# Pointwise weights loaded as 256 + 128 rows around the first input block, and one weight piece evicted by two engines

## The chip, the cores and the metric

The kernel runs on one core of one Trainium2 chip. The metric is the device time of one execution in microseconds (us); the median of several runs is compared.

## What is computed

A depthwise separable convolution with a 1x1 depthwise kernel, in bf16. `x` is (1, 384, 384, 384), that is 147,456 pixels of 384 channels; `dw` is (1, 1, 384) and `pw` is (384, 384):

```python
out = x * dw[0, 0][None, None, None, :]      # k = 1: no neighbours, no padding
return jnp.einsum('bhwc,cd->bhwd', out, pw)
```

So it is one matrix product of 147,456 x 384 by 384 x 384, whose weights are `pw` with row c scaled by `dw[c]`.

## The kernel before

**Tiling.** The pixels are cut into 288 supertiles of 512. Chunks of 1 to 10 supertiles are loaded by one DMA each into three rotating buffers X; the first two chunks, x0 and x1, are one supertile each, the next two have two, then one has four, and from there on most have ten. For each supertile VectorE (DVE in the profile) transposes 32x32 blocks of 32-bit words from X to T (L369; for the very first supertile block by block, L367), the tensor engine (PE) multiplies, and ScalarE (ACT) evicts the result from PSUM to O (L429), from where SyncE's queue (SP) stores it.

**The main stream.** `supertile(s, rv)` issues 12 steps `(b, par)` of four matmuls each, one for each quarter q of the partitions, all at L225. The weights are the moving operand `w_r[:, b, par, :]`, T the stationary one. Results go to the PSUM buffer PS[0] for even supertiles and PS[1] for odd ones, one bank per q. `w_first` lists which weight evictions a step of an even supertile waits for: those of pieces 0 to 3 before step (0,0), piece 4 before (4,0), piece 5 before (4,1), which are the ninth and eleventh steps. `s_tb` makes steps (1,0) and (2,0) wait for blocks 1 and 2 of the first transpose.

**The weights.** Because the transpose works on pairs of channels, the rows of `pw` are spread to another order and scaled by `dw` on PE. `pw` lies in `raw` as three parts k of 128 rows. For each k and r in 0, 1, a pair of matmuls (L275, v = 0 and 1, each on 64 rows of the array and each into a bank of its own) makes weight *piece* i = 2k + r in two PSUM banks: pieces 2 and 3 in PS[0], the others in PS[1]. The left operand `sel_w` is a 0/1 selection times `dw`, made by DVE (L400) from a transposed `dw` row (L255). `times` repeats a pair: the same matmuls again into the same banks, with the piece's mark `s_w` after the last. `w_out(i)` evicts piece i from PSUM into `w_r` (L385); the engine is `w_eng[i]`, 0 for DVE and 1 for ACT, and `s_wr[e]` counts what each engine has evicted. Pieces 4 and 5 use the banks of pieces 0 and 1 and wait for their eviction (L272).

**Order at the start.** Each engine works through its instructions in the order written.
- SP's queue: `pw` part 0 (L179), `pw` parts 1 and 2 (L180), x0, x1 and the following chunks (L133). The first stores are held by 28 waits on `s_pw` (L195).
- PE: `idle_work(4)`, the `dw` row, `idle_work(2)`, the six pieces, then the main stream. `idle_work(n)` issues n sets of four matmuls on constants (L242); nothing reads what they write.
- DVE: the selection, `sel_w`, its piece, then the transposes of supertiles 0 and 1.
- ACT: its pieces in order, then the output evictions.
- GpSimd (POOL) copies some weights for the last supertile once all pieces are out (`w_all`, L329 to L333).

## Time and profile before

| | |
|---|---|
| median of 5 runs | 573.95 us (573.62 to 574.03) |
| profiled execution, its own time | 574.21 us |
| its span (first to last profiled instruction) | 572.2 us |
| granted clock in the page | 9 in all 40 slices (90% of full speed or more) |
| PE / PEld (weight loads) | 566.8 us (99%) / 417.0 us (73%) |
| DVE / ACT / POOL | 507.3 us (89%) / 418.7 us (73%) / 13.9 us (2%) |
| DMA | 226.88 MB, mean 397 GB/s |
| first matmul of the main stream | 6.39 us |

PE is the matmul row and PEld its weight loads, which overlap it; matmul ends are modelled. L12 is line 12 of the kernel. An entry such as "0.3 <-ACT w_r L385" says that the engine stood for 0.3 us until the instruction named released it. The chain of waits follows the work that ended last back to its start. The timeline merges equal instructions that follow one another. SPq and ACTq are the DMA issues of those engines.

### The profile page before, as it was taken

How to read it: one execution, taken by the hardware profiler on the slowest of the kernel's cores; microseconds unless marked ns; L12 is line 12 of the kernel's file. 1: busy time of each engine (PE TensorE's matmuls, PEld its weight loads, DVE VectorE, ACT ScalarE, POOL GpSimd, SP SyncE). 2: the span in 40 equal slices, each digit the busy share in tenths (PEclk: the TensorE clock that was granted, in tenths of full speed). 3: DMA queues.
4: the chain of work that ended last, by engine and by line, in shares of the span. 5: the costliest groups of instructions: out<-in, count | busy, mean ns of one | idle time of the engine just before them, and what ended most of it. 6: DMA issues, size and time to landing. Idle time of an engine off the chain costs nothing.

```text
span 572.2 us, 29707 instructions
## 1 busy us (share of the span) xinstructions
PE 566.8 (99%) x13843; PEld 417.0 (73%) x13843; DVE 507.3 (89%) x588; ACT 418.7 (73%) x298; POOL 13.9 (2%) x41
## 2 busy tenths in 40 slices
PE   8999999999999999999999999999999999999997
PEld 5777777777777777777777777777777777777774
DVE  6899899899999999999999999999999999999995
ACT  6777777777777777777777777777777777777775
POOL 2042000000000000000000000000000000000000
PEclk9999999999999999999999999999999999999999
DMA  8999999999999999999999999999999999997877
GB/s 343 428 389 422 424 417 425 434 425 416 431 420 424 380 399 430 399 381 396 427 394 383 419 422 414 395 412 428 388 390 423 410 380 395 425 396 301 341 286 255
DMA packets 26740, 226.88 MB, mean 397 GB/s; under 512 B 1385, under 2 KB 7274, under 8 KB 22890
## 3 DMA queue, kind: packets, MB, share of 16 engines
q1 hardware_dynamic: 25796, 225.91, 97.5%
q10 hardware_dynamic: 934, 0.89, 0.4%
q14 instruction: 9, 0.07, 0.0%
q8 instruction: 1, 0.02, 0.0%
HBM read 113.54 MB, written 113.25 MB: 396 GB/s over the span
## 4 chain that ended last, share of the span: by engine, by line
PE 99%; ACT 0%; issue 0%
PE ps L225 98%; ACT w_r L385 0%; PE ps L242 0%; PE ps L310 0%; PE ps L298 0%; PE ps L275 0%; ACT O L424 0%; PE ps L255 0%
## 5 line engine op out<-in xcount | busy, mean ns | idle before, releaser
L225 PE MATMUL ps<-w_r,T 32*128 32x384 bf16 x13776 | 559.8, 321 | 0.3 <-ACT w_r L385 0.3
L369 DVE STREAM_TRANSPOSE T<-X 128x384 uint32<-128x384 uint32 x571 | 499.4, 878 | 55.8 <-DMA X<-in_x_dram 2.9
L225 PEld LDWEIGHTS ps<-w_r,T 32*128 32x128 bf16 x13776 | 414.4, 93 | 145.7 <-issue 0.6
L429 ACT CAST O<-ps 128x1536 bf16<-128x1536 f32 x286 | 411.7, 1440 | 146.4 <-PE ps L225 146.4
L339 POOL COPY Xk<-Xl 32x256 bf16<-32x256 bf16 x16 | 6.3, 394 | 0.0
L338 POOL COPY Xk<-Xl 32x128 bf16<-32x128 bf16 x16 | 4.6, 288 | 25.2 <-DMA Xl<-in_x_dram 24.4
L385 ACT CAST w_r<-ps 128x768 bf16<-128x768 f32 x5 | 3.6, 818 | 0.9 <-PE ps L275 0.9
L333 POOL COPY raw<-w_r 32x768 bf16<-32x768 bf16 x4 | 3.3, 820 | 6.5 <-ACT w_r L385 6.4
L242 PE MATMUL ps<-const-bfloat16-1.0 32*128 32x384 bf16 x24 | 2.3, 512 | 1.1 <-PEq L454 1.1
L275 PE MATMUL ps<-raw 64*128 64x384 bf16 x16 | 2.6, 466 | 0.1
L341 ACT ACT_TABLE_LOAD x1 | 1.3, 1283 | 1.5 <-PEq L454 1.5
L275 PEld LDWEIGHTS ps<-raw 64*128 64x128 bf16 x16 | 0.8, 111 | 2.2 <-DMA raw<-in_pw_dram 1.2
L420 DVE CAST O<-ps 128x384 bf16<-128x384 f32 x2 | 1.0, 552 | 1.4 <-PE ps L225 1.4
L369 DVE STREAM_TRANSPOSE T<-Xl 128x384 uint32<-128x384 uint32 x2 | 1.8, 882 | 0.2
L242 PEld LDWEIGHTS ps<-const-bfloat16-1.0 32*128 32x128 bf16 x24 | 0.6, 117 | 1.4 <-issue 1.4
L390 DVE TENSOR_REDUCE sel<-eye 128x64 f32<-128x128 bf16 x1 | 0.3, 290 | 1.5 <-POOL eye L320 1.5
L352 DVE STREAM_TRANSPOSE T<-Xk 128x384 uint32<-128x384 uint32 x2 | 1.2, 578 | 0.5 <-PE ps L225 0.4
L424 ACT CAST O<-ps 128x384 bf16<-128x384 f32 x2 | 1.0, 480 | 0.7 <-PE ps L310 0.7
L310 PE MATMUL ps<-raw,T 128*128 128x384 bf16 x8 | 1.5, 327 | 0.0
L385 DVE CAST w_r<-ps 128x768 bf16<-128x768 f32 x1 | 1.0, 958 | 0.5 <-PE ps L275 0.5
L424 DVE CAST O<-ps 128x384 bf16<-128x384 f32 x2 | 1.1, 558 | 0.1
L419 ACT CAST O<-ps 128x384 bf16<-128x384 f32 x2 | 0.9, 482 | 0.5 <-PE ps L225 0.5
(14 smaller groups left out, 5.1 us busy)
## 6 DMA issues: line engine op xcount, KB each, us to landing
X<-in_x_dram SPq DMA_DIRECT2D x26, 3840.0 KB, 22.2
out_dram<-O SPq DMA_DIRECT2D x26, 3840.0 KB, 28.2
X<-in_x_dram SPq DMA_DIRECT2D x3, 1536.0 KB, 19.5
out_dram<-O SPq DMA_DIRECT2D x4, 768.0 KB, 8.3
out_dram<-O SPq DMA_DIRECT2D x2, 1536.0 KB, 14.0
X<-in_x_dram SPq DMA_DIRECT2D x1, 2304.0 KB, 21.2
out_dram<-O SPq DMA_DIRECT2D x1, 2304.0 KB, 12.1
X<-in_x_dram SPq DMA_DIRECT2D x4, 384.0 KB, 4.9
```

What stands on the lines that cost most here:

```text
L225: mm = nc.tensor.matmul(PS[s][:, q, :D], lhsT=Ts[s][32 * q : 32 * q + 32, b, par::2], rhs=w_r[32 * q : 32 * q + 32, b, par, :], start=(b, ...
L242: nc.tensor.matmul(PS[0][:, 2 * (i % 2) + i // 2, :D], lhsT=ones[32 * i : 32 * i + 32, 0:P], rhs=ones[32 * i : 32 * i + 32, :], start=True ...
L275: mm = nc.tensor.matmul(PS[(k + 1) % 2][:, 2 * r + v, :D], lhsT=sel_w[64 * v : 64 * v + 64, k, r, :, :].rearrange("p q w -> p (q w)"), rhs ...
L310: mm = nc.tensor.matmul(PS[1][:, m, :D], lhsT=Tk[:, P * (m + 2) : P * (m + 3), par], rhs=w_k[:, par, :], start=False, stop=par == 1,)
L333: nc.gpsimd.tensor_copy(w_k[quads[n]], w_r[quads[n], n]).then_inc(s_wk)
L338: nc.gpsimd.tensor_copy(Xk[quads[n], g:8:4, :], x_b).then_inc(s_xk)
L339: nc.gpsimd.tensor_copy(Xk[quads[n], 8 + g : 24 : 4, :], Xl[quads[g], :, 64 * n : 64 * n + 64]).then_inc(s_xk)
L341: nc.scalar.copy(warm[:, s : s + 1], nc.const_aps.tensor(0.0, [P, 1], F32)).then_inc(s_a[s])
L369: ins = nc.vector.transpose(out=Tw[:, 3 * h : 3 * h + 3], in_=Xw[:, :, j, 96 * h : 96 * h + 96].rearrange("p k (b w) -> p b k w", w=32),)
L385: o = nc.vector.tensor_copy(out, in_) if e == 0 else nc.scalar.copy(out, in_)
L424: o = (nc.scalar.copy if n % 2 else nc.vector.tensor_copy)(Ov[:, n, j, :], PS[s][:, n, :D])
L429: a = nc.scalar.copy(Ov[:, :, j, :], PS[s][:, :, :D])
```

## The change

`pw`'s parts 0 and 1 come in one first DMA, counted by `s_pw`; then x0; then part 2, counted by `s_pw2`, for which PE now waits before k = 2 and not before k = 1. One more set of idle matmuls is issued, piece 3's pair is issued twice, and those of pieces 4 and 5 are issued once. Piece 3 is evicted by two engines: bank 0 by ACT in its old place, bank 1 by DVE between blocks 0 and 1 of the first transpose. The counts that others wait for follow. In total the same bytes are loaded by as many DMAs.

```diff
         w_eng = [1, 0, 1, 1, 1, 1]
-        w_all = [(s_wr[e], w_eng.count(e)) for e in range(2)]
+        w_all = [(s_wr[0], 2), (s_wr[1], 5)]

         nc.scalar.dma_start(dw_row[:], dw.rearrange("a e c -> a (e c)")).then_inc(s_dw, 16)
-        nc.sync.dma_start(pw_n[:, 0], pw[0:P, :]).then_inc(s_pw, 16)
-        nc.sync.dma_start(pw_n[:, 1:3], pw[P:C, :].rearrange("(k p) d -> p k d", p=P)).then_inc(s_pw2, 16)
+        nc.sync.dma_start(pw_n[:, 0:2], pw[0 : 2 * P, :].rearrange("(k p) d -> p k d", p=P)).then_inc(s_pw, 16)
         load_x(0)
+        nc.sync.dma_start(pw_n[:, 2], pw[2 * P : C, :]).then_inc(s_pw2, 16)
...
-        w_first = {(0, 0): [(0, 1), (1, 3)], (4, 0): [(1, 4)], (4, 1): [(1, 5)]}
+        w_first = {(0, 0): [(0, 2), (1, 3)], (4, 0): [(1, 4)], (4, 1): [(1, 5)]}
...
-        idle_work(2)
+        idle_work(3)
         nc.tensor.wait_ge(s_pw, 16)
-        times = {(2, 0): 2, (2, 1): 2}
+        times = {(1, 1): 2}
         for k in range(3):
-            if k == 1:
+            if k == 2:
                 nc.tensor.wait_ge(s_pw2, 16)
             nc.tensor.wait_ge(s_sw, k + 1)
...
                         nc.vector.transpose(out=Tw[:, b], in_=x_b).then_inc(s_tb if b else s_t[0][0])
+                        if b == 0:
+                            w_out(3, 1)
                     continue
...
-        def w_out(i):
+        def w_out(i, bank=0):
             e, k, r = w_eng[i], i // 2, i % 2
             out, in_ = w_r[:, 2 * k : 2 * k + 2, r, :], w_ps(i)
+            if i == 3:
+                out, in_ = out[:, bank], in_[:, bank]
+                e = 1 - bank
             o = nc.vector.tensor_copy(out, in_) if e == 0 else nc.scalar.copy(out, in_)
```

## The prediction

> **What bounds the kernel now.** I read the page first: its chain of waits and its groups of instructions.

> ```profile
> PE 99%; ACT 0%; issue 0%
> PE ps L225 98%; ACT w_r L385 0%; PE ps L242 0%; PE ps L310 0%; PE ps L298 0%; PE ps L275 0%; ACT O L424 0%; PE ps L255 0%
> ...
> L225 PE MATMUL ps<-w_r,T 32*128 32x384 bf16 x13776 | 559.8, 321 | 0.3 <-ACT w_r L385 0.3
> ```

> The main stream of matmuls (L225) is 559.8 us of a span of 572.2, and once it runs it never waits: its whole idle time is the 0.3 us before its first matmul, ended by a weight eviction on ACT. So the change can move the end in three ways only: the stream starts earlier or later, it stalls, or its matmuls run slower.

> Next, the chain in order of time, asked for the first 12 us (start, duration, what):

> ```profile
> 3.51 0.52 PE ps L275 x2
> 4.03 0.02 issue
> 4.05 2.21 ACT w_r L385 x3
> 6.26 0.14 issue
> 6.39 5.68 PE ps L225 x133
> ```

> The stream starts at 6.39, 0.14 after ACT's third eviction (pieces 0, 2 and 3, chained from 4.05). All four pieces must be out before it: supertile 0 writes the PSUM buffer that holds pieces 2 and 3.

> Last, the timeline of the start-up (start, duration, engine, work, idle before it and its releaser), and of DVE at 9 to 10.3 us:

> ```profile
> 3.48 0.16 PEld L275 LDWEIGHTS ps<-raw 64*128 64x128 bf16 x4 [0.74 <-DMA raw<-in_pw_dram]
> 4.05 3.61 ACT L385 CAST w_r<-ps 128x768 bf16<-128x768 f32 x5 [0.93 <-PE ps L275]
> 4.07 0.20 PEld L275 LDWEIGHTS ps<-raw 64*128 64x128 bf16 x4 [0.44 <-DMA raw<-in_pw_dram]
> 4.37 0.96 DVE L385 CAST w_r<-ps 128x768 bf16<-128x768 f32 x1 [0.48 <-PE ps L275]
> 5.53 0.70 DVE L367 STREAM_TRANSPOSE T<-X 128x128 uint32<-128x128 uint32 x3 [0.20 <-DMA X<-in_x_dram]
> ...
> 9.22 1.58 DVE L369 STREAM_TRANSPOSE T<-X 128x384 uint32<-128x384 uint32 x2 [0.89 <-DMA X<-in_x_dram]
> ```

> DVE is done with piece 1 at 5.33 and stands 0.20 until x0 lands at 5.50, while ACT still has piece 3 to do. At 9.22 DVE again has only just got its input: the third supertile's X.

> **The change, part by part.** The sum is made on the profiled run: 574.21 us, its span of 572.20 and 2.01 around it. That is 0.26 above the median of 573.95, so a shift found here is taken off the median.

> *First load, 192 KB for 96.* Before, 96 KB issued at 0.95 landed 2.0 later (2.95), and the 192 KB issued at 1.41 landed 2.6 later (4.03). Bounds for 192 KB issued first: 2.95 and 0.95+2.6=3.58. By packets: the DMA view counts 139 up to 2.50 us, 14 of them under 512 B, about the 128 of the first load, which landed 0.45 later; up to 2.98 it counts 273, 17 of them small, the 256 that the new load has. 2.98+0.45=3.43, or a little under: I take 3.4. The row from landing to matmul is 4.03 to 4.10, so the pieces could start at 3.47; before they started at 3.51, held by sel_w (DVE L400, the first ending at 3.36). The load costs nothing; at its upper bound, 0.14.

> *A third idle_work set.* Each set takes about 0.3 (2.55, then 2.85), so it is issued at about 3.17 and its streaming ends at 3.49 to 3.55 (the last quadrant started late, at 2.91). Beside the wait for the load it costs 0 to 0.04; I charge 0.02.

> *The wait before k=1 taken away.* It ended at 4.03 and the matmuls ran at 4.10. But a pair of L275 takes 0.32 at that clock and the pair before started at 3.78, so 4.10 is when PE was free anyway. The gap of 0.44 on PEld is a hidden one. Gain: nothing.

> *Piece 3 issued twice.* Its pair at 4.42 is repeated at 4.74, so its mark moves from 4.97 to about 5.29. ACT comes to piece 3 at 5.43 and DVE later, so they hide it. Without that cover it would cost up to 0.32.

> *Piece 3 split.* ACT's evictions start 0.69 apart (4.05, 4.74, 5.43). Bank 0 is 128x384; the nearest rows are ACT's output evictions of that shape, 480 and 482 ns: ACT ends at 5.43+0.48+0.02=5.93 for 6.25. Bank 1 goes to DVE behind piece 1 (ends 5.33+0.02) and block 0. DVE's rows for 128x384 out of PSUM are 552 and 558 ns.

> *x0 behind 192 KB for 288.* Issued at 1.41 for 1.87, so up to 0.46 earlier; or by bytes, 98 KB at the 294 GB/s of the stretch from 2.5 to 5.5, 0.33 earlier. That is 5.04 to 5.17 for 5.50; unmoved is the upper bound. Below 5.35 it no longer counts, as DVE isn't free. Block 0 then starts at 5.35, bank 1 0.23 later (blocks started at 5.53 and 5.76) at 5.58, and ends at 6.14; if it overlaps the end of piece 1 by the 0.08 that consecutive DVE rows show, 6.06. I take 6.10. If x0 doesn't move: 5.53+0.23+0.56=6.32.

> *The start.* The last release is DVE's at 6.10 for ACT's at 6.25; 0.14 to the first matmul as before, and 0.03 for the wait on ACT's count that now follows it: 6.27 for 6.39, **0.12 earlier** (0.2 earlier to 0.1 later between the ends).

> *pw's last 96 KB behind x0.* It stands where x0 stood, with the same bytes up to its end: 5.5. Bounds: 96 KB behind x0's earliest 5.04 at 294 GB/s, 5.37; or behind an unmoved x0 at the pace of the old second load (192 KB in 1.08 after the first, so 0.54), 6.04. This wait is new, and in PE's queue all of the main stream stands behind it. 5.55+0.07=5.62, then two pairs (the doubled ones are gone) of 0.32 at the old clock: PE is free at 6.26, just inside 6.27. At the upper bound 6.04+0.07+0.64=6.75, 0.36 later than before.

> *Behind them on ACT:* pieces 4 and 5 at about 6.1 to 6.95 and 6.8 to 7.65; the stream asks for them 8 and 10 steps of 0.163 after its start, 7.57 and 7.90. Hidden with 0.25 to spare.

> *Blocks 1 and 2 and the next transpose on DVE* come about 0.3 later against piece 1's end than they could: 6.05, 6.25 and 6.45, ending by 7.0. The stream asks 0.33, 0.65 and 0.98 after 6.27. Hidden; from 0.3 more it would show.

> *What is late next.* The third supertile's X lies behind the same bytes as before, so its transpose still ends at 10.09 (9.22+0.88); the PEld row started 0.07 after that, at 10.16, and a matmul can follow 0.03 later, 10.19. Before, PE came there at 10.29. So no more than **0.10** of the start is kept. The next transposes have over half a microsecond.

> Sum: -0.12 at the start, 0.02 given back at 10.2: **-0.10, 573.85 us**, well inside the 0.2% (1.15 us) that a measurement of this kernel can tell from no change.

> **Rule and row on the clock.** The rows: L275 matmuls that started from 5.0 to 5.3 took 474 to 517 ns, those from 5.6 to 5.8 took 322 to 360, and L225 takes 321 throughout. So the doubling of PE's pace fell at about 5.6, 4.5 us after the first matmul at 1.12. In the 3.4 us before it PE stood (pairs and sets counted at 0.32) at 2.37-2.53, 3.2-3.5 and 4.74-4.99, 0.7 us in all. After the change the middle one is filled and the last becomes 5.06 to 5.6: 0.16+0.54, again 0.7 us. I take it that the pace doubles at the same time.
> [...]

> **Rivals.**
> - *The pause restarts the clock's warm-up* (slower). PE waits for pw's last load from 5.06 to 5.6. If what counts is unbroken work, the 4.5 us from the first matmul start anew at 5.6 and the stream runs at 0.32 a step until 10.1. Half of the time from 6.27 on is lost: 1.9, less the 0.10, so 575.75. A switch that is only partly late gives less: it is slower by over 0.2% from a switch at about 9.0 on, (9.0-6.27)/2-0.10=1.27. For it: the new pause is twice as long as the old last one. Against: the total in the same stretch is unchanged and the old pauses did not prevent the switch. 0.17.
> - *The loads give it back.* pw's last part lands near 6.0, or the first near 3.6, or x0 hardly moves: the stream starts 0.1 to 0.4 later, 574.05 to 574.35. For it: the chain PE-free 6.26 against 6.27 has no slack. Against: the same bytes had landed at 5.50. 0.19.
> - *More than the sum*: x0 early, bank 1 done by 6.0, and the third X early by 0.15: -0.2 to -0.35, 573.6 to 573.75. Nothing can give over 0.2%, as the stream can't start before bank 0 is out at 5.93. 0.05, of it 0.01 beyond.

> **How the numbers follow.** The forecast has 0.59; its own range is 573.6 to 574.1 (the start's bounds of -0.2 and +0.1, and runs that spread from 573.62 to 574.03). The range takes in the second rival, the third, and that part of the clock's case in which the switch comes by 9.0 or so: 573.4 to 575.2. Faster 0.01; slower 0.17, all of it the clock; within 0.2% 0.82.

> **What would show it.** Right: the first L225 matmul at about 6.25 with DVE's 128x384 cast of L385 as the releaser in place of ACT; DVE's L367 with no wait for x0; PEld's second wait on raw ending at 5.5 and not at 4.03; the third supertile waiting a little for DVE L369; L225 at 321 ns from its start. Wrong: L225 rows of about 500 ns at the start, or a first L225 matmul that follows directly on L275 after 6.4.

## The result: slower by 0.16%, and the times spread

The median is 574.70 us (573.83 to 576.47, 26 runs) against 573.95 us (573.38 to 574.95, 47 runs) before; ratio 1.0016, 95% interval 1.0011 to 1.0021. That is inside the 0.2% that the prediction calls no change, but clear of no difference, and on the other side of the forecast of 573.85. The median moved by 0.75; the largest time moved by 1.5. Of the 26 runs 18 lie between 573.8 and 574.8 (mean 574.42), none between 574.8 and 575.3, and 8 from 575.3 to 576.5 (mean 575.84). The mean of before is 573.93, so the lower group costs 0.5 and the upper 1.9.

The profiled execution took 575.79 us, its span 574.1, and is of the upper group. Its page, for the lines shown of before:

```profile
PE 98%; DMA 1%; SPq 0%; ACT 0%; issue 0%; POOLq 0%
PE ps L225 98%; DMA raw<-in_pw_dram 1%; PE ps L310 0%; PE ps L275 0%; PE ps L298 0%; ACT O L429 0%; SPq L179 0%; SPq L133 0%; SPq L470 0%; POOLq L113 0%; POOLq L459 0%
...
L225 PE MATMUL ps<-w_r,T 32*128 32x384 bf16 x13776 | 561.7, 322 | 0.0
```

A DMA of `pw` has come into the chain, ACT's weight evictions have left it, and the main stream is busy for 1.9 us more than the 559.8 of before without any wait. The chain of the first 12 us says where the DMA stands:

```profile
1.97 4.04 DMA raw<-in_pw_dram
6.01 0.05 issue
6.06 0.82 PE ps L275 x4
6.88 5.23 PE ps L225 x65
```

`pw`'s last 128 rows, issued at 1.97, landed at 6.01; then pieces 4 and 5, then the stream. The timeline (start, duration, idle before and its releaser) has the details:

```profile
4.41 0.96 DVE L390 CAST w_r<-ps 128x768 bf16<-128x768 f32 x1 [0.67 <-PE ps L275]
5.29 0.30 DVE L367 STREAM_TRANSPOSE T<-X 128x128 uint32<-128x128 uint32 x1
5.51 0.52 DVE L390 CAST w_r<-ps 128x384 bf16<-128x384 f32 x1
5.95 0.49 DVE L367 STREAM_TRANSPOSE T<-X 128x128 uint32<-128x128 uint32 x2
6.05 0.13 PEld L275 LDWEIGHTS ps<-raw 64*128 64x128 bf16 x4 [1.41 <-DMA raw<-in_pw_dram]
6.06 0.82 PE L275 MATMUL ps<-raw 64*128 64x384 bf16 x4 [0.72 <-DMA raw<-in_pw_dram]
6.81 9.36 PE L225 MATMUL ps<-w_r,T 32*128 32x384 bf16 x180
8.98 0.86 DVE L371 STREAM_TRANSPOSE T<-X 128x384 uint32<-128x384 uint32 x1 [0.90 <-PE ps L225]
```

DVE did what the change is for: it no longer waits for x0, and its bank was out at 6.03. But PE had to wait for the load, and the stream starts at 6.81, 0.42 later than before. The last row is the second loss: DVE now waits for PE in a stretch where before it waited for a load. The matmuls of L225 in two stretches of this profile, 6.8 to 10.5 us and from 11 us on (ns, least, median, most):

```profile
L225 PE MATMUL ps<-w_r,T x48: 492/522/523, 6.8 to 10.3; 32*128 32x384 bf16 x48
...
L225 PE MATMUL ps<-w_r,T x228: 321/321/321, 10.8 to 19.9; 32*128 32x384 bf16 x114
```

The stream ran its first 12 steps at 0.32 each in place of 0.163. The windows view from 7 to 9 us (stretch, length, busy time and count of PE, PEld, DVE, ACT and POOL, then PEclk, DMA share and GB/s), first of the changed kernel, then of the kernel before:

```profile
7.00:9.00 2.00, 2.00 (x28) 0.92 (x24) 1.06 (x3) 1.10 (x2) 0.75 (x1) 1.00 1.02 424
```

```profile
7.00:9.00 2.00, 2.00 (x57) 1.45 (x50) 1.04 (x2) 1.08 (x2) 1.14 (x2) 1.00 1.01 418
```

PE reads as fully busy in both and did half the matmuls in one; the column PEclk does not show it, the count does. The trace's record of the granted clock does: full from 10.65 us here, from 5.65 before. So this execution lost 0.42 at the start and (10.65-6.81)/2=1.92 by the clock; its last L225 matmul started at 568.18 for 565.90, 2.28 later. What follows that matmul took 0.4 less (5.9 for 6.3 to the end of the span).

### The profile page after: what moved, and what is told of

Read it like the earlier page. It is cut to its first block, busy times and chain, and to the rows that moved or that the text cites. A ratio compares the mean times of both kernels' runs of the same rounds, so it can differ in the third digit from the quotient of the medians.

```text
span 574.1 us, 29711 instructions
## 1 busy us (share of the span) xinstructions
PE 568.7 (99%) x13845; PEld 340.4 (59%) x13845; DVE 507.8 (88%) x589; ACT 418.5 (73%) x298; POOL 13.9 (2%) x41
## 4 chain that ended last, share of the span: by engine, by line
PE 98%; DMA 1%; SPq 0%; ACT 0%; issue 0%; POOLq 0%
PE ps L225 98%; DMA raw<-in_pw_dram 1%; PE ps L310 0%; PE ps L275 0%; PE ps L298 0%; ACT O L429 0%; SPq L179 0%; SPq L133 0%; SPq L470 0%; POOLq L113 0%; POOLq L459 0%
## 5 line engine op out<-in xcount | busy, mean ns | idle before, releaser
L225 PE MATMUL ps<-w_r,T 32*128 32x384 bf16 x13776 | 561.7, 322 | 0.0
L225 PEld LDWEIGHTS ps<-w_r,T 32*128 32x128 bf16 x13776 | 337.6, 93 | 224.3 <-issue 2.6
L390 ACT CAST w_r<-ps 128x768 bf16<-128x768 f32 (+1 forms) x5 | 3.4, 741 | 1.6 <-PE ps L275 1.6
L242 PE MATMUL ps<-const-bfloat16-1.0 32*128 32x384 bf16 x28 | 2.5, 516 | 1.1 <-PEq L459 1.1
L275 PE MATMUL ps<-raw 64*128 64x384 bf16 x14 | 2.6, 516 | 0.7 <-DMA raw<-in_pw_dram 0.7
L275 PEld LDWEIGHTS ps<-raw 64*128 64x128 bf16 x14 | 0.7, 124 | 2.5 <-DMA raw<-in_pw_dram 2.0
L390 DVE CAST w_r<-ps 128x768 bf16<-128x768 f32 (+1 forms) x2 | 1.5, 739 | 0.7 <-PE ps L275 0.7
L242 PEld LDWEIGHTS ps<-const-bfloat16-1.0 32*128 32x128 bf16 x28 | 0.9, 121 | 1.5 <-issue 1.4
L310 PE MATMUL ps<-raw,T 128*128 128x384 bf16 x8 | 1.5, 327 | 0.0
L424 ACT CAST O<-ps 128x384 bf16<-128x384 f32 x2 | 0.9, 482 | 0.5 <-PE ps L225 0.5
```

What stands on the lines that cost most here:

```text
L225: mm = nc.tensor.matmul(PS[s][:, q, :D], lhsT=Ts[s][32 * q : 32 * q + 32, b, par::2], rhs=w_r[32 * q : 32 * q + 32, b, par, :], start=(b, ...
L242: nc.tensor.matmul(PS[0][:, 2 * (i % 2) + i // 2, :D], lhsT=ones[32 * i : 32 * i + 32, 0:P], rhs=ones[32 * i : 32 * i + 32, :], start=True ...
L275: mm = nc.tensor.matmul(PS[(k + 1) % 2][:, 2 * r + v, :D], lhsT=sel_w[64 * v : 64 * v + 64, k, r, :, :].rearrange("p q w -> p (q w)"), rhs ...
L310: mm = nc.tensor.matmul(PS[1][:, m, :D], lhsT=Tk[:, P * (m + 2) : P * (m + 3), par], rhs=w_k[:, par, :], start=False, stop=par == 1,)
L390: o = nc.vector.tensor_copy(out, in_) if e == 0 else nc.scalar.copy(out, in_)
```

## The experiments

Theory A: the wait for `pw`'s last part costs twice, by a later start and by a pause of PE that makes the full clock come late in some runs. Theory B: only the late load counts, not the pause as such. Theory C: the split of piece 3 costs. Theories D and E are named where they arise. Each ratio is to the kernel before, timed in the same session: its medians there were 573.87 to 574.04, and 5 of its 106 runs lie above 575, up to 576.30.

**Filling the pause** (in the changed kernel, before k = 2):

```diff
             if k == 2:
+                nc.tensor.wait_ge(*w_done[0])
+                for v in [0, 1] * 3:
+                    nc.tensor.matmul(PS[1][:, v, :D], lhsT=ones[64 * v : 64 * v + 64, 0:P],
+                                     rhs=ones[64 * v : 64 * v + 64, :], start=True, stop=True,
+                                     tile_position=(64 * v, 0))
                 nc.tensor.wait_ge(s_pw2, 16)
```

> The changed kernel with PE's pause before pw's last part filled: three pairs of matmuls on constants into piece 0's two banks, after piece 0 is evicted. Nothing else moves: in the changed kernel's profile PE stands from about 5.1 to 6.06 us, and three pairs are 0.96. Theory A (the stream starts 0.4 late, and the pause besides makes PE's pace double late, at 10.6 in that profile): the late start stays (first L225 at about 6.8), but the pace is doubled by 7.3 in every run, so the times draw together near 573.95+0.4=574.35, none above 575. Theory B (only the late load and the split of piece 3 matter, the pause as such does not): median and spread as the changed kernel's, 574.7 with runs up to 576.5.

Median 574.83 (574.67 to 575.69, 11 runs); ratio to before 1.0019, interval 1.0010 to 1.0028. The chain of its profile:

```profile
3.62 1.72 PE ps L285 x10
5.33 0.96 PE ps L270 x6
6.29 0.64 PE ps L285 x4
6.93 4.29 PE ps L225 x96
```

L270 are the added matmuls, L285 the pieces. The times drew together: 9 of 11 within 0.4 us, where the changed kernel spread over 2.6. But they drew together 0.5 above what was expected, and three runs lie above the 575 that theory A named as the limit (575.05, 575.50, 575.69). In this run `pw`'s last part landed at 5.42, so the filling itself held PE until 6.09 and kept the start at 6.87 where a start near 6.25 was to be had. The two losses come apart: without the pause most of the spread goes and the late start stays. What made the two slowest runs slow is not shown.

**The last part on ACT's queue:**

```diff
-        nc.sync.dma_start(pw_n[:, 2], pw[2 * P : C, :]).then_inc(s_pw2, 16)
+        nc.scalar.dma_start(pw_n[:, 2], pw[2 * P : C, :]).then_inc(s_pw2, 16)
```

> The changed kernel with pw's last part issued on ACT's queue behind dw, at about 1.5 us, in place of SP's behind x0. Theory A: it lands at 4.5 to 5.2, the wait at 6.01 is gone, PE's pause shrinks to under 0.6, the stream starts at about 6.3 as the prediction had it, and the time is 573.85, runs within 573.4 to 574.6. Theory C (the split of piece 3 between ACT and DVE is what costs): the stream still starts after 6.5 or waits later, and the time stays at 574.4 or more. x0 may land some 0.2 later than the 4.38 of the changed kernel; DVE does not ask for it before 5.3.

Median 574.62 (573.76 to 575.94, 11 runs), ratio 1.0018, interval 1.0009 to 1.0027. In the profile (573.76 us) the part landed at 4.66 and the stream started at 6.32, behind DVE's bank, near the 6.27 of the prediction's sum:

```profile
4.41 0.96 DVE w_r L390
5.37 0.26 DVE T L367
5.63 0.45 DVE w_r L390
6.08 0.24 issue
6.32 5.68 PE ps L225 x130
```

DVE's bank was out at 6.08 for the 6.10 of the sum, and from there to the first matmul 0.24 passed for 0.17. The start is not after 6.5, as theory C had it, though the median is over the 574.4 that it named. The runs split into two groups, six from 573.8 to 574.6 and five from 575.5 to 575.9, with nothing between. Their means lie 1.6 us apart, which does not look like a load that lands now a little earlier, now a little later.

**A pause and nothing else** (the kernel before):

```diff
-        idle_work(2)
+        idle_work(0)
```

> The kernel before with its second call of idle work (two sets, 8 matmuls, 2.55 to 3.23 us) left out; all loads and evictions as they were. The first piece waits for sel_w as before, so the stream still starts at 6.39. Theory A (a pause of about 1 us within the 3.4 us stretch that decides on PE's pace makes the doubling late): slower by 0.6 to 1.0 in the median (574.5 to 574.9), runs up to 576, and in the profile a first L225 matmul at about 6.4 that takes some 500 ns. Theory B (pauses as such do not matter): 573.95 with the spread of before.

Median 574.64 (573.79 to 575.58, 11 runs), ratio 1.0011, interval 1.0001 to 1.0020. Loads, evictions and repeats are those of before, and the stream started at 6.26, even 0.13 earlier (PE, timeline):

```profile
3.37 2.95 PE L275 MATMUL ps<-raw 64*128 64x384 bf16 x16 [0.73 <-DVE raw L400]
6.26 0.51 PE L225 MATMUL ps<-w_r,T 32*128 32x384 bf16 x4
```

Its profile is the quickest of its runs, so the slow first matmuls that were expected show only from 6.26 to 6.67. The kernel's median rose by 0.77 by the loss of eight matmuls whose results nobody reads. Theory B falls.

**The split alone** (kernel before, with `w_out(3, 1)`, the new counts and nothing else of the change):

> The kernel before with only the eviction split: bank 0 of piece 3 on ACT, bank 1 on DVE between blocks 0 and 1 of x0. Loads, idle work and repeats as before. x0 lands at 5.50, so bank 1 is out at about 6.25 and the stream starts at 6.35 to 6.45. Theory A: no change beyond 0.1 us from 573.95, no wider spread. Theory C (the split costs): slower by 0.3 or more, with the start of the stream later than 6.6 or a stall behind it.

Median 574.21 (573.82 to 575.45, 11 runs), ratio 1.0007, interval 0.9998 to 1.0016: not settled. x0 landed at 5.65, DVE's bank was out at 6.43 and the stream started at 6.68, both about 0.2 to 0.3 later than expected. The signs that theory C named are there, a start after 6.6 and a median 0.34 above before, but the interval holds no change. In this place the split needs x0 early.

**The order of loads alone** (kernel before, with the new load order and the wait at k = 2):

> The kernel before with only the order of the loads changed (256 rows of pw, x0, last 128 rows; PE's wait for the last part moved to k=2); eviction, idle work and repeats as before. PE stands from 4.8 (piece 3 once) until pw's last part lands at 5.4 to 6.0, then issues four pairs (1.28 us at the slow pace). Theory A (late start and late doubling of PE's pace, both from the wait for pw's last part): the stream starts at 6.8 to 7.4, some runs miss the doubling, median 574.6 to 575.3, spread to 576 or more. Theory C (the split of piece 3 costs): as before, 573.95.

Median 575.32 (573.98 to 576.44, 12 runs), ratio 1.0020, interval 1.0010 to 1.0030; 7 of 12 above 575.2. This part alone is enough for a loss of the size of the whole change; the intervals overlap, so that it costs more is not shown. Its profile (574.85 us) shows a third way to lose. `pw`'s last part landed at 5.55 and the full clock came early, at 4.53, so the four pairs took half the time expected and the stream started at 6.36, before the 6.8 of theory A. But x1 landed at 8.23, and the stream had to wait for it (PE, timeline):

```profile
5.60 0.82 PE L275 MATMUL ps<-raw 64*128 64x384 bf16 x8 [0.80 <-DMA raw<-in_pw_dram]
6.36 2.13 PE L225 MATMUL ps<-w_r,T 32*128 32x384 bf16 x48
8.98 0.51 PE L225 MATMUL ps<-w_r,T 32*128 32x384 bf16 x8 [0.49 <-DVE T L369]
```

**ACT's queue, with the repeats moved to pieces 4 and 5:**

```diff
-        times = {(1, 1): 2}
+        times = {(2, 0): 2, (2, 1): 2}
```

> The changed kernel with pw's last part on ACT's queue and the repeats moved from piece 3 to pieces 4 and 5, so that PE is busy from 3.55 to about 6.2 and the stream starts at 6.32. In the run with ACT's queue alone PE stood from 5.77 to 6.32 and 5 of 11 times lay near 575.7, six near 574.1. Theory A (a pause within the deciding 3.4 us makes the doubling of PE's pace late by a whole such stretch, 1.7 us of time): the upper group is gone, all runs between 573.6 and 574.5, median 573.8 to 573.95. Theory D (the upper group comes from ACT's queue, e.g. a late load or late evictions): it stays, median over 574.3.

Median 574.53 (574.06 to 576.54, 12 runs), ratio 1.0014, interval 1.0003 to 1.0026; 4 of 12 above 575.2. The expectation failed: the upper group stayed. In the profiled run (575.62) `pw`'s part landed at 5.48 on ACT's queue and x0 at 6.21, so PE stood from 4.84 to 5.53 and again until 7.24, and the full clock came at 9.30. ACT's queue does not make the load sure: 5.48 here for the 4.66 above. Theory D's sign, that the group stays, is there, and late loads with it. In this run they lengthen the pause, and the shares in the table below fit the pause as the cause of the late clock; that the other slow runs have the same cause is not shown.

**One more idle set in the kernel before:**

```diff
-        idle_work(2)
+        idle_work(3)
```

> The kernel before with one more set of idle matmuls (idle_work(3) in place of 2), which fills the pause from 3.23 to 3.51; nothing else changed, so the stream starts at 6.39 to 6.45. Theory A: the doubling of PE's pace is never later than 7.5, so the upper tail of the times of before (574.4 to 576.1) shrinks and the median is 573.8 to 573.95. Theory B (pauses do not matter): 573.95 or, if the set holds up the first piece, up to 0.1 more, with the same tail.

Median 574.12 (573.73 to 574.35, 12 runs), ratio 0.9998, interval 0.9990 to 1.0007: no gain in the middle, since PE now ends the pieces at 6.30 and the stream starts at 6.44. But no run lies above 574.35, where 7 of the 29 runs of before beside it do.

**The changed kernel, profiled again:**

> The changed kernel, profiled once more, to see whether its parts vary from run to run. Theory A: the first L225 matmul follows pw's last part by 0.75 to 0.8 us wherever that lands (6.01 and 6.81 in the first profile), and the pace doubles either by 7.3 (time 573.8 to 574.8) or not before 9 (575.3 to 576.5). Theory B: pw's last part lands at 6.0 again and the pace doubles at 10.6 again.

574.62 us. The last part landed at 5.77, the stream started at 6.57, 0.80 after it; full clock from 7.14. The chain shows one more loss, small, before the third supertile:

```profile
6.64 4.28 PE ps L225 x96
10.92 0.17 issue
11.09 2.92 PE ps L225 x65
```

The third chunk's X had landed at 10.02, not at 9.1. So a run of the lower group: 0.18 by the start, (7.14-6.57)/2=0.28 by the clock, 0.17 by the third chunk, 0.63 in all, and its time is 0.67 above the median of before.

**`pw`'s last part ahead of x0** (changed kernel, these two lines swapped):

> The changed kernel with pw's last 128 rows loaded ahead of x0 (still as 256 and 128 rows, on SP's queue). Theory A (the place behind x0 is what makes the last part late and opens the pause): it lands at about 4.0 as pw's second load did before, PE runs on until 5.8, and x0 lands at 5.5 to 5.7, so DVE's bank is out at 6.3 to 6.45 and the stream starts at 6.4 to 6.7, PE standing for 0.6 to 0.9 before it: most runs at 574.0 to 574.4, a few still at 575.5 to 576. The loads behind (third chunk) land at 9.1 to 9.5 as before, not at 10.0. Theory E (the form of the first load, 256 rows, is what makes all later loads late): the third chunk lands near 10 again and the time stays at 574.6 or more.

Median 574.55 (573.96 to 576.36, 11 runs), ratio 1.0016, interval 1.0007 to 1.0025; 8 runs up to 574.9 and 3 from 575.8 up. The last part landed at 4.55 and no longer held PE; x0 landed at 5.54, and the stream started at 6.57, 0.80 after PE's last pair. The third chunk landed at 8.38, so theory E falls for this run. The pause has only moved, from behind piece 3 to behind piece 5, and with it the upper group stays.

**A candidate:** the loads of before; piece 3 split, with the counts and the new `w_out` of the change, and with DVE's bank straight behind piece 1, where DVE waits for x0 anyway; three idle sets; only piece 5 repeated. Beside the kernel before:

```diff
         for i in range(6):
             w_out(i)
+            if i == 3:
+                w_out(3, 1)
...
-        idle_work(2)
+        idle_work(3)
...
-        times = {(2, 0): 2, (2, 1): 2}
+        times = {(2, 1): 2}
```

> A candidate from the runs so far: the loads of the kernel before, a third set of idle matmuls, piece 3 split, but with DVE's bank directly behind piece 1 and ahead of x0's blocks (DVE stands there until x0 lands at 5.5), and only piece 5 issued twice. Theory A: ACT's bank is out at about 5.97, DVE's at 5.88, block 0 at 6.1, PE is busy until 6.1, so the stream starts at 6.25 to 6.3 and PE's pace is never doubled later than 7.3; 573.8 to 573.95 with no run above 574.5. Theory C (the split itself costs): a start later than 6.4, or a median above 574.1.

> The candidate with the loads of the kernel before, a third idle set, DVE's bank of piece 3 ahead of x0's blocks and only piece 5 issued twice, measured once more, since its first interval (0.9988 to 1.0006) holds no change. If the earlier start (6.18 for 6.39) is kept: again 573.7 to 573.9 and 0.1 below the kernel before, the start at 6.2 and the pace doubled by 7.3. If the third chunk's late landing takes it back (9.92 in the first profile, PE standing for 0.26 at 10.7): 573.95, no different from before.

Twice: 573.83 (573.28 to 574.49, 11 runs), ratio 0.9997, interval 0.9988 to 1.0006; and 573.82 (573.41 to 574.43, 11 runs), ratio 0.9995, interval 0.9986 to 1.0004. Both medians lie 0.11 to 0.14 below the kernel before and both intervals hold no change, so a gain is likely and not shown. The start at 6.18 was there in both profiles. In the first the third chunk landed at 9.92 and took it back:

```profile
6.24 4.49 PE ps L225 x84
10.73 0.26 issue
10.99 3.08 PE ps L225 x69
```

In the second it landed at 9.22 and nothing was taken back. No run of the 22 lies above 574.5.

**The candidate with the first load as 256 rows** (256 and 128 rows, both ahead of x0):

> That candidate with pw loaded as 256 and 128 rows, both ahead of x0, and the wait for the second part at k=2. In the run with this order alone the chunks behind x0 landed at 6.5 and 8.4, earlier than the 7.1 and 9.1 to 9.9 with 128 and 256 rows. Theory A: pw's last part lands at about 4.5, before piece 3 is through (4.8), so there is no pause; x0 at 5.5, the stream starts at 6.2 to 6.25, the third chunk is no longer late, and all of the 0.15 to 0.2 is kept: 573.75, no run above 574.5. Theory E (256 rows in the first load make later loads late): 574.2 or more.

Median 574.37 (573.81 to 576.51, 12 runs), ratio 1.0008, interval 0.9997 to 1.0020; 3 of 12 above 575.2. The expectation failed. x0 landed at 6.47 in the profiled run and the stream waited for it until 6.91:

```profile
1.96 4.51 DMA X<-in_x_dram
...
6.50 0.32 DVE T L367
...
6.91 7.14 PE ps L225 x169
```

So theory E's sign is there for this kernel, as x0 landed late; in the kernel of the same load order above it landed at 5.54. Two profiles cannot say how often.

**What the profiles say of the clock together.** Each of the fourteen traces has one record of the full clock, from its grant to its end, 2.3 to 5.4 us after the start of the last matmul (4.30 in the kernel before, 3.61 in the changed one). In twelve it is 566.61 us long, in the changed kernel and the one with ACT's queue and moved repeats 563.20. To the nanosecond the records are 566.612 us in the kernel before and 563.199 in the changed one: 3.413 apart, and 166.02 and 165.02 times that difference. From these lengths comes the estimate that the rest of this section uses: the full clock began and ended at points 3.413 us apart. No experiment moved such a point. Against the kernel's start the grants lie at no fixed place: what their times leave after division by 3.413 runs from 0.25 (the grant at 7.08) to 3.26 (the one at 6.67). The two executions with the shorter record are also the only profiled ones above 575 us, and the only ones with the full clock later than 7.3. For nine profiles the table gives the share of time in which PE's array was fed (each set or pair of matmuls counted at 0.32 from its start, the stream as always busy) in the 3.413 us before the grant, and in the 3.413 us before that, at whose end no grant came. Time before the first matmul, at 1.12, counts as standing.

| kernel | time | longest pause of PE | stream from | full clock from | share before the grant | share in the 3.413 us before that |
|---|---|---|---|---|---|---|
| before | 574.21 | 0.28 | 6.39 | 5.65 | 0.81 | 0.33 |
| changed | 575.79 | 0.93 | 6.81 | 10.65 | 1.00 | 0.69 (and 0.75 before it) |
| changed, again | 574.62 | 0.69 | 6.57 | 7.14 | 0.76 | 0.72 |
| pause filled | 574.67 | 0.14 | 6.87 | 7.26 | 0.96 | 0.76 |
| ACT's queue | 573.76 | 0.55 | 6.32 | 6.65 | 0.80 | 0.62 |
| ACT's queue, repeats moved | 575.62 | 0.69 | 7.24 | 9.30 | 0.87 | 0.75 |
| last part ahead of x0 | 574.31 | 0.80 | 6.57 | 7.21 | 0.77 | 0.74 |
| idle work left out | 573.79 | 0.98 | 6.26 | 6.67 | 0.86 | 0.37 |
| one more idle set | 574.18 | 0.23 | 6.44 | 7.08 | 0.89 | 0.71 |

In these and the other five the lowest share before a grant is 0.758, and the highest in a stretch without one 0.759; the count is good to about 0.01. So about 0.76 divides the two, which is an estimate from the fourteen traces and holds only if the stretch is taken to end at the grant. By it, the worst position that a stretch behind the first matmul can have in the kernel before (ending at 6.4, over the pauses from 3.2 on) has 0.77: barely enough. In the changed kernel the worst position (ending at 6.8) has 0.65, and so has the worst with idle work left out (ending at 4.9). In the changed kernel's first profile two stretches (0.75 and 0.69) went by without a grant, and the stream ran at 0.32 a step for 0.163 from 6.81 to 10.65, which is the 1.92 above; one stretch of 3.413 us at that pace is up to 1.7 us of time. Laid over all positions, a limit of 0.76 makes the first profile of the changed kernel lose so in about 4 of 10 cases, and the second in 1 to 5, as its worst stretches lie right at the limit (estimates from their pauses); 8 of 26 runs were in the upper group. The candidate's worst positions have 0.83, and none of its runs was there. Not every kernel fits by its one profile: in that of ACT's queue alone no position has under 0.79 and in that of the filled pause none under 0.9, so by the estimate none should lose, but 5 and 2 of their 11 runs lie above 575.4. Either PE stood longer in those runs than in the profiled one (x0 landed at 5.29 and 6.21 in the two profiles with ACT's queue), or something else delays them; this stays open.

That pauses of PE cost time by themselves is shown by the kernel that leaves out idle matmuls and nothing else (574.64 for 573.87); the one with a set more points the same way, but no run of 12 against 7 of 29 can be chance. That they do so by the clock is read from the traces, one execution of each kernel. The share of 0.76 is read from the fourteen traces too and was not set by an experiment of its own.

## Why the prediction was wrong

*Right, by its steps.* The first load landed at 3.37 (3.4 was taken) and cost nothing beside the third idle set: the pieces began at 3.55 for 3.51. The wait taken away was worth nothing: k = 1 at 4.16, later than 4.10. The repeat of piece 3 was hidden. ACT's bank was out at 5.98 (5.93), DVE's at 6.03 (6.10); where the load did not interfere the stream started at 6.32 and, with DVE's bank moved forward, at 6.18. One term was short there: from DVE's release to the first matmul 0.24 to 0.26 passed in four profiles (ACT's queue with and without the moved repeats, the split alone, the last part ahead of x0), for the 0.17 taken over from ACT's release. The third chunk was what is late next: 0.17 in the changed kernel's second profile, 0.26 in the candidate's.

*The step that failed is "pw's last 96 KB behind x0".* It was taken at 5.5, "with the same bytes up to its end". In the profiles with this order it landed at 6.01, 5.77, 5.55 and 5.42, and x0 ahead of it at 4.38 to 5.04, no later than the earliest that the prediction allowed. The upper end of 6.04 was right as a bound; the value was not, because equal bytes did not give equal landings. With 128 and 256 rows first, the third load in line landed at 5.45 to 5.65 in six profiles; with 256 rows first, the third load landed at 5.42 to 6.47 in the six profiles that keep it on SP. From 4.0 to 5.0 us the changed kernel moved under 200 GB/s, and so did the three other profiles with this order (151 to 194) (stretch, then as above; the last number is GB/s):

```profile
4.00:4.50 0.50, 0.50 (x8) 0.17 (x4) 0.09 (x1) 0.41 (x1) 0.00 (x0) 1.00 0.96 163
4.50:5.00 0.50, 0.50 (x6) 0.14 (x2) 0.50 (x1) 0.50 (x2) 0.00 (x0) 1.00 0.73 192
```

The kernel before moved 375 and 277 there; its own trough was earlier, 186 to 267 from 2.0 to 4.0, under work that did not wait for it. Why the trough moves and what makes it longer in some runs stays open.

*The step that failed with it is the count of pauses.* The prediction set the pause at 0.54, found 0.7 us of standing in the same 3.4 us before and after, and took the clock's switch as unchanged. Two things were wrong. The pause follows the load one for one, so 6.01 made it 0.93 and 5.77 made it 0.69; the rivals "the loads give it back" and "the clock" were given chances as if apart, but the same late load brought both. And the stretch was laid in one place, the one of the profile shown. No row of the kernel before shows its length of 3.4 us; the 3.413 above is the difference of two records, one of them of the changed kernel. Nor did the full clock keep its place: it came at 5.65 us before, and at 10.65 and 7.14 in the two profiles of the changed kernel. By the estimate above, the worst place that the stretch can have says whether some runs lose.

*The rival's size was right, its mechanism was not.* It had 1.9 lost by the clock, from 6.27 to 10.1, and 575.75; the profiled run lost 1.92, from 6.81 to 10.65, and took 575.79. But unbroken work of 4.5 us is not what counts: in the second profile of the same kernel the pause of 0.69 ended at 5.82 and the full clock came at 7.14. That the numbers lie so close is luck, as the profiled run is near the latest grant that its pauses allow (10.7 by the estimate above). The 9.0 from which it counts a late switch as slower is no grant of any run: later than 7.3 the full clock came in two profiles, at 9.30 and 10.65. Its chance of 0.17 was too low for something that hits 8 runs in 26, and the mixture moves the median by less than 0.2%, which the prediction, with one outcome for all runs, had no place for: it was about 0.5 in the 18 runs that kept the clock and 1.9 in the 8 that did not.

## What to carry to other kernels

When a load is moved behind another, ask not only when it lands but what stands idle until then, and whether that engine's pace depends on its having been busy. Where the full clock comes now early and now late, as here at 4.53 us in one profile and at 10.65 in another, count the engine's pauses for the worst position of the stretch before it, not for the profiled one, and keep a margin: matmuls that nobody reads were worth 0.8 us of the median here. A median that moves little with a spread that grows from 1.6 to 2.6 us can be a sign of two outcomes; look at the list of times before the profile, since one profile shows only one of them.
